# Attention and two MoE layers on one core: a pick made for two tiles at once, a lent token-mix matrix, and a conversion that runs one frame earlier

## The chip, the cores and the metric

The kernel runs on one core of one Trainium2 chip. The metric is device time in microseconds (us). The kernel before took 875.06 us (median of three runs, 874.54 to 876.78).

## What is computed

Sparse attention over 4 batches and 8 heads (576 tokens, 64 wide) keeps the 32 largest scores of a row; a soft mixture of 8 experts and a two-layer MLP follow. Cut to what matters:

```python
scores = q @ k.T / 8                       # per batch and head, 576 x 576
kth    = np.partition(scores, -32)[..., -32]
attn   = softmax(where(scores >= kth, scores, -1e9)) @ v
x      = attn laid out as (2304, 512)
logits = x @ phi                           # 32 slots: 8 experts of 4
slots  = softmax(logits, over tokens).T @ x
out_e  = relu(slots_e @ w1[e]) @ w2[e]     # 8 experts, 512 -> 1024 -> 512
y      = softmax(logits, over slots) @ out_e
h      = y @ w_in                          # 512 -> 2048
g      = h if h >= 1, 0 if h <= -1, else (h + 1)**2 / 4
result = g @ w_out                         # 2048 -> 512
```

## The kernel before

**Stages.** Attention runs over 16 pairs of heads (one pair is two heads of one batch). Then come the experts: `h` (siT times w1, L804), `so` (times w2, L823), the token-mix matrix (`mix`, L757 to L793, written to `cT`), and the MLP (`h_ps` L898, `o_ps` L916).

**A pair** has 1,152 score rows, that is nine tiles of 128 rows: row groups 0 to 3 have two tiles each (j = 0 and 1), row group 4 has one. A tile goes through these steps; a word such as `K31` is step K of row group 3, tile 1.

- S: scores on TensorE (L311) into `s_ps`, of which there are two buffers. C: copy to `ssb` in SBUF on ScalarE (L329).
- G: the eight largest of each of seven segments, on VectorE (L338). L: three rounds on these 56 candidates give the 24 largest in order (L343, L345).
- M: the mask of scores not below the 24th, with a count of them in `cnt_all`. It runs on VectorE (L398), and for the tiles in `MASK_POOL` on GpSimd (L396), whose count ScalarE makes (O, L406).
- X: the scores once more into an `s_ps` buffer (L311), from which a matmul of the mask (L413) takes a huge number wherever the mask is set. Y: the eight largest of what is left (L422, `l`).
- K: the 32nd largest is picked from these eight, by the count. `rank8` holds 31, 30, ..., 24; where it equals the count, the value is kept and summed into `kb`. This is one instruction for a tile, L431, that compares, multiplies and adds up; the sum is fetched by a second one, an accumulator read.
- B (GpSimd, L438), P (ScalarE, L442), U (GpSimd, L445), E (ScalarE, L448) turn the tile into exponentials; T, Q, R, A, H (L457 to L507) transpose it and multiply it by v.

**Order.** The list `ORDER` (L58 to L68) is written by hand and sets the order on TensorE, ScalarE, VectorE and GpSimd through attention. The loop over frames (L710 to L713) emits, for each word, the step of pair frame - k, where the word's last letter gives k (a is 0, b is 1, c is 2). So a frame does the first steps of one pair, the middle steps of the pair before and the last ones of the pair before that. Each pair's step K has nine words; K00 to K11 stand in the pair's own frame, K20 to K40 in the next one. The words `z0` to `z4` prepare the next pair's q and k (copies on ScalarE, differences on GpSimd at L284 and L286, and DMAs). Words `md` and `mc` run pieces of the experts' logits in some frames.

**Conversion.** 16 blocks of w_in are made from 64-bit to 32-bit numbers, one a pair, by the words `c0` to `c6` (ScalarE L213 to L217, GpSimd L219, L223, L225, VectorE L221, load L192, store L205). Their letters are b and c: a pair's block is converted one and two frames after its first steps.

**Weight loads.** 88 loads of 512 KB stand in one list: 64 for w1 and w2, then the converted w_in and w_out. A load needs a free slot in SBUF. At first 13 slots `wA` are free, and each frame may issue two loads (`wload(2)`, at S00). When the last pair begins, six slots of the q and k buffers come free, later others; after the frames the conversion's two (`cv_slots`) and four halves (`half_slots`). What is left waits until `h` and `so` have read a slot: load i takes the slot of an earlier one, in the order of the list `ring`. SP issues all loads, in order.

After the frames, a scheduler orders each engine's work.

Of the kernel before, what the change touches and what calls it, by code (L numbers as in the profile page):

```python
# [8 lines left out]
F32 = mybir.dt.float32  # L9
F32R = mybir.dt.float32r  # L10
# [4 lines left out]
ALU = mybir.AluOpType  # L15
# [4 lines left out]
P = 128  # L20
# [38 lines left out]
Y30b z4b E00b Q30c A11c X21b P11b T40c S00a md M31b H1c A20c Y21b Q31c K20b c4c U01b E01b C00a  # L59
G00a K21b K30b c2c L4b S01a Q40c U11b N3b C01a R4c X31b Y31b A21c E10b S10a T00b T01b G01a B2b  # L60
c5c P21b M40b H2c P20b E11b C10a K31b L0a O40b U21b S11a C11a Q00b A30c N0a B3b M00a X40b G10a
Q01b U20b R0b P30b G11a Y40b L1a M10a A31c T10b S20a H3c T11b c6c E20b E21b R1b N4b S21a M01a
# [3 lines left out]
z3a H0b G31a S40a c0b T30b M21a c1b K11a L3a E40b T31b mc B0a P00a O21a mc c3b R3b C40a  # L66
# [7 lines left out]
def kernel_body(tc, qT, kT, vP, phi, w1, w2, w_in, w_out, out, fast, flag):  # L74
# [8 lines left out]
    cT = cpool.tile([P, NT], F32R, name="cT")  # L83
# [37 lines left out]
    def whole(pool, tag, bufs):  # L121
        return ((pool, tag, bufs),)
# [8 lines left out]
    wfree = list(slots_a)  # L131
# [9 lines left out]
    def wload(n):  # L141
        while n > 0 and wfree and wnext[0] < len(worder):
# [5 lines left out]
            ring.append(slot)  # L148
# [275 lines left out]
    def op_k(u, j):  # L424
        t = st[u]["t0"] + j
        if j == 0:
            st[u]["kb"] = p_small.tile([P, 2], F32, name="kb", tag="kb")
            st[u]["pick"] = p_small.tile([P, 2, 8], F32, name="pick", tag="pick")
        kth = st[u]["kb"][:, j:j + 1]
        if fast:  # L430
            nc.vector.scalar_tensor_tensor(st[u]["pick"][:, j], rank8, cnt_all[:, t:t + 1], st[u]["l8"][:, j],  # L431
                                           op0=ALU.is_equal, op1=ALU.mult, accum_out=kth)
        else:
            nc.vector.tensor_copy(kth, st[u]["top"][:, j, TOPK - 1:])
# [213 lines left out]
    def emit(name, pi):  # L648
        k = name[0]
        if k == "l":  # L650
            op_late(pi, name[1])
        elif k == "z":
            op_split(pi + 1, int(name[1]))
        elif k == "m":
            if pi % NHP == NHP - 1:
                op_moe(pi, k)
        elif k in "cd":
            if k == "c" or pi < NWE:
                i = pi + min(pi, NWE) + (k == "d")
                if i < NCV:  # L660
                    conv_op(i, int(name[1]))
        else:
            if name == "G00" and pi > 0:
                return
            if name == "S00":
                wload(2)
            if pi == NPAIR - 1 and last_pair(name, pi):
                return
            calls[k]((pi, int(name[1])), *([int(name[2])] if len(name) > 2 else []))
            if pi == NPAIR - 1:  # L670
                last_op(name)
# [42 lines left out]
    wfree.extend(cv_slots + half_slots)  # L714
# [41 lines left out]

    def mix():  # L757
        wide = [P, NR + 1, B, NSLOT]
# [20 lines left out]
        for b in range(B):  # L779
# [6 lines left out]
            for rows in (range(NR), (NR,)):  # L786
                ps = ps_m.tile([P, NR, P], F32, name="c_ps", tag="m_ps")
                for r in rows:
                    n = P if r < NR else REM
                    nc.tensor.transpose(ps[:, r % NR, :n], c4[:n, r].rearrange("p a b s -> p (a b s)"), ident[:n, :n])  # L790
                w = len(rows) * n
                nc.scalar.copy(cT[:, b * S + rows[0] * P:b * S + rows[0] * P + w],
                               ps.rearrange("p a b -> p (a b)")[:, :w])  # L793
# [101 lines left out]
    def emit_g(s_):  # L895
        t, f = s_
        ph = ps_m.tile([P, 512], F32, name="h_ps", tag="m_ps")[:, :BLK]
        nc.tensor.matmul(ph, m4[f // 4][:, f % 4 * P:(f % 4 + 1) * P], cT[:, t * BLK:(t + 1) * BLK], start=True, stop=True)  # L898
# [110 lines left out]
```

## Time and profile before

| what | us |
|---|---|
| median of three runs | 875.06 |
| the three runs | 874.54, 876.78, 875.06 |
| span of the profiled execution | 872.0 |
| two startup frames | 0 to 68 |
| frames of the other pairs | 68 to about 527 |
| end of attention, logits of the last batch | 527 to 568.8 |
| experts, mixing, first part of w_out's conversion | 568.8 to 640 |
| rest of the conversion of w_out, first MLP steps | 640 to 710 |
| rest of the MLP | 710 to 872 |

Of the profiled execution only its span is known; the median of the runs is 3.1 us above it (launch and end of the program lie outside the span). Frames are of three kinds: eight plain ones of 31.5 us (from 68.0, 99.6, 131.1, 231.5, 263.0, 363.4, 394.9 and 495.3), three with the words `md` of 35.3 us (from 162.6, 294.5 and 426.4), and three with the words `mc` of 33.6 us (from 197.9, 329.8 and 461.7). The starts named here lie one repeat of TensorE's pattern apart.

### The profile page before, as it was taken

The numbers are of one execution on the slowest core, as the hardware profiler recorded it, in microseconds if no ns is written. First come the engines' busy times: TensorE is split into PE (matmuls) and PEld (weight loads), VectorE is DVE, ScalarE is ACT, GpSimd is POOL, SyncE is SP. The second block draws the span as 40 slices with busy tenths as digits, with TensorE's granted clock in tenths as the row PEclk, the third lists the DMA queues.
The fourth block names the chain that finished last, engine by engine and source line by source line (L and its number), as shares of the span: only waits on it lengthen the run. The fifth ranks groups of instructions, "written<-read, shape, count | busy, mean of one in ns | idle before, by whom it ended". The sixth has DMA issues, their size and how long they took to land.

```text
span 872.0 us, 17711 instructions
## 1 busy us (share of the span) xinstructions
PE 821.5 (94%) x5695; PEld 674.7 (77%) x5695; DVE 685.8 (79%) x3084; ACT 644.8 (74%) x1292; POOL 485.4 (56%) x494
## 2 busy tenths in 40 slices
PE   4889999999999999999999999799698899999996
PEld 3678989988989988988988988632266678888885
DVE  6999999988999989999989994103389995666663
ACT  5688999988998988998988987412578766545453
POOL 2577888877888877888877774100467740000000
PEclk9799999999999999999999999899799999999999
DMA  8453563553353353353452536699940001001001
GB/s 240 124 152 96 165 176 98 156 157 89 103 142 92 112 133 89 102 142 87 117 134 78 157 101 205 206 343 386 399 175 1 0 2 73 37 0 38 1 37 40
DMA packets 49461, 108.59 MB, mean 125 GB/s; under 512 B 8304, under 2 KB 8304, under 8 KB 49360
## 3 DMA queue, kind: packets, MB, share of 16 engines
q1 hardware_dynamic: 49040, 106.73, 40.2%
q8 instruction: 47, 0.77, 0.4%
q10 hardware_dynamic: 320, 0.66, 0.3%
q14 instruction: 54, 0.44, 0.2%
HBM read 70.70 MB, written 8.91 MB: 91 GB/s over the span
## 4 chain that ended last, share of the span: by engine, by line
PE 78%; DVE 10%; DMA 6%; ACT 3%; POOL 1%; issue 1%; ACTq 0%; POOLq 0%; SPq 0%; DVEq 0%
PE s_ps L311 20%; PE o_ps L916 17%; PE av_ps L485 14%; PE pt_ps L457 7%; PE s_ps L413 4%; PE av_ps L486 3%; PE rem_ps L230 3%; DMA w<-in_moe_w_dram 2%; DMA w<-in_moe_w_out_dram 2%; PE h L804 2%; DVE cand L338 2%; PE moe_ps L569 2%; DMA w<-cv_d 1%; PE h_ps L898 1%; PE xT_ps L534 1%
## 5 line engine op out<-in xcount | busy, mean ns | idle before, releaser
L311 PE MATMUL s_ps<-kh,q 128*128 128x288 f32 x640 | 208.1, 342 | 16.4 <-DVE q L266 9.0
L916 PE MATMUL o_ps<-whl,ghl 128*128 128x512 f32 x864 | 216.9, 395 | 5.0 <-DVE ghl L904 4.0
L916 PEld LDWEIGHTS o_ps<-whl,ghl 128*128 128x128 f32 x864 | 159.1, 188 | 44.7 <-DVE ghl L904 7.1
L445 POOL TENSOR_TENSOR ssb<-ssb,pen 128x576 f32<-128x576 f32 x141 | 180.4, 1284 | 18.3 <-ACT pen L442 15.8
L311 PE MATMUL s_ps<-kl,q 128*128 128x288 f32 x640 | 181.2, 299 | 0.0
L338 DVE MAX8 cand<-ssb 128x8 f32<-128x82 f32 (+1 forms) x1008 | 164.2, 228 | 5.0 <-ACT ssb L329 4.0
L311 PEld LDWEIGHTS s_ps<-kh,q 128*128 128x128 f32 x640 | 123.6, 193 | 34.7 <-DVE q L266 9.4
L485 PE MATMUL av_ps<-v_sb,ptb 128*128 128x65 f32 (+1 forms) x1280 | 147.1, 261 | 0.4 <-ACT xT L547 0.4
L485 PEld LDWEIGHTS av_ps<-v_sb,ptb 128*128 128x128 f32 (+1 forms) x1280 | 141.1, 181 | 5.2 <-issue 2.6
L311 PEld LDWEIGHTS s_ps<-kl,q 128*128 128x128 f32 x640 | 124.4, 194 | 0.3
L422 DVE MAX8 l<-s_ps 128x8 f32<-128x576 f32 x144 | 109.2, 758 | 18.3 <-PE s_ps L413 17.9
L442 ACT ACTIVATE pen<-ssb,kb 128x576 bf16<-128x576 f32 x141 | 110.3, 792 | 4.5 <-POOL kb L438 3.3
L329 ACT COPY ssb<-s_ps 128x576 f32<-128x576 f32 x144 | 91.1, 641 | 25.3 <-PE s_ps L311 21.8
L448 ACT ACTIVATE ssb<-ssb,nm 128x576 f32<-128x576 f32 x141 | 109.0, 785 | 0.6 <-POOL ssb L445 0.6
L900 ACT ACTIVATE rg<-h_ps,half 128x384 f32<-128x384 f32 x96 | 55.2, 579 | 71.0 <-PE h_ps L898 70.8
L396 POOL TENSOR_SCALAR mb<-ssb,top 128x576 bf16<-128x576 f32 x48 | 83.3, 1736 | 19.2 <-DVE top L345 9.2
L902 DVE SCALAR_TENSOR_TENSOR rg<-h_ps,rg 128x384 f32<-128x384 f32 x96 | 52.9, 554 | 47.4 <-ACT rg L901 47.1
L467 ACT COPY ptb<-pt_ps 128x512 f32<-128x512 f32 x144 | 82.4, 598 | 3.3 <-PE av_ps L485 3.3
L457 PE MATMUL pt_ps<-ident,ssb 128*128 128x128 f32 x576 | 84.3, 273 | 0.2
L398 DVE TENSOR_SCALAR_CACHE_REDUCE mb<-ssb,top 128x576 bf16<-128x576 f32 x96 | 75.8, 802 | 0.0
L345 DVE MAX8 top<-cand 128x8 f32<-128x56 f32 x432 | 73.5, 207 | 0.1
L457 PEld LDWEIGHTS pt_ps<-ident,ssb 128*128 128x128 f32 x576 | 68.7, 142 | 1.3 <-ACT ptb L467 0.8
(160 smaller groups left out, 1311.7 us busy)
## 6 DMA issues: line engine op xcount, KB each, us to landing
w<-in_moe_w_dram SPq DMA_DIRECT2D x60, 512.0 KB, 6.7
q<-qst SPq DMA_DIRECT2D x60, 160.0 KB, 3.1
kh<-kst SPq DMA_DIRECT2D x60, 144.0 KB, 2.5
kl<-kst SPq DMA_DIRECT2D x60, 144.0 KB, 2.9
x<-in_moe_w_in_dram SPq DMA_DIRECT2D x16, 512.0 KB, 3.9
w<-in_moe_w_out_dram SPq DMA_DIRECT2D x16, 512.0 KB, 9.3
v_sb<-in_v_dram SPq DMA_DIRECT2D x16, 325.0 KB, 2.9
raw_t<-in_q_dram SPq DMA_DIRECT2D x15, 320.0 KB, 3.7
```

The source lines that it names most:

```text
L311: nc.tensor.matmul(s[:, hf, :HS], a, w, start=(n == 0), stop=(n == len(terms) - 1), skip_group_check=True)
L329: nc.scalar.copy(st[u]["ssb"][:, j], st.pop((u, j))[:, :, :HS])
L338: nc.vector.max(st[u]["cand"][:, j, 8 * g:8 * g + 8], row(u, j)[:, S * g // NSEG:S * (g + 1) // NSEG])
L396: nc.gpsimd.tensor_scalar(st[u]["mb"][:, j], row(u, j), t_u, None, op0=ALU.is_ge)
L422: nc.vector.max(st[u]["l8"][:, j], st.pop((u, j))[:, :, :HS])
L442: nc.scalar.activation(pen, row(u, j), AF.Relu, bias=st[u]["kb"][:, j:j + 1], scale=-BIG)
L445: nc.gpsimd.tensor_tensor(row(u, j), row(u, j), st.pop((u, "pen", j)), op=ALU.subtract)
L448: nc.scalar.activation(row(u, j), row(u, j), AF.Exp, bias=st[u]["nm"][:, j:j + 1], scale=0.125)
L457: nc.tensor.transpose(pt[:, c, :], pr[:, c * P:(c + 1) * P], ident)
L467: nc.scalar.copy(ptb, st.pop((u, "pt", j)))
L485: nc.tensor.matmul(o, pj[:, c, sl], v_sb[:, 4 * jj + c, :], start=(c == 0), stop=False)
L916: nc.tensor.matmul(pos[t][n], a[:, sl], w, start=(f == 0 and k == 0), stop=(f == NF - 1 and k == 2))
```

## The change

Four edits.

- **Pick.** `op_k` does nothing for the first tile of a row group. At the group's last tile it picks for both: a compare of `rank8` with the counts (128x16), a multiply by `l8` (128x16), and a sum over each tile's eight (128x2). Three instructions, the second and third of which use what the one before wrote. Row group 4 has one tile and takes three instructions too (128x8). Per pair, nine picks of two instructions each (18) become five of three (15).
- **Lent matrix.** `cT`, 9 KB a partition, was allocated for the whole kernel and is written by `mix` only. It becomes two tiles in a pool of its own, which are two more slots for the first two weight loads. They are not put in `ring`.
- **Conversion one frame earlier.** The letters of c0, c1 and c3 change from b to a, those of c2, c4, c5 and c6 from c to b.
- **Slots of the conversion.** `cv_slots` are given to weight loads after the last block's c6, which now stands in the last pair's next frame, instead of after all frames.

```diff
-G00a K21b K30b c2c L4b S01a Q40c ...     (c4c c5c c6c c2c -> b; c0b c1b c3b -> a)
+G00a K21b K30b c2b L4b S01a Q40c ...
...
-    cT = cpool.tile([P, NT], F32R, name="cT")
+    p_ct = ctx.enter_context(tc.tile_pool(name="p_ct", bufs=1))
...
-    wfree = list(slots_a)
+    loan = [whole(p_ct, f"cT{n}", 1) for n in range(2)]
+    wfree = loan + slots_a
...
-            ring.append(slot)
+            if slot not in loan:
+                ring.append(slot)
...
     def op_k(u, j):
-        t = st[u]["t0"] + j
-        if j == 0:
-            st[u]["kb"] = p_small.tile([P, 2], F32, name="kb", tag="kb")
-            st[u]["pick"] = p_small.tile([P, 2, 8], F32, name="pick", tag="pick")
-        kth = st[u]["kb"][:, j:j + 1]
+        n, t = width[u[1]], st[u]["t0"]
+        if j < n - 1:
+            return
+        kb = st[u]["kb"] = p_small.tile([P, 2], F32, name="kb", tag="kb")
         if fast:
-            nc.vector.scalar_tensor_tensor(st[u]["pick"][:, j], rank8, cnt_all[:, t:t + 1], st[u]["l8"][:, j],
-                                           op0=ALU.is_equal, op1=ALU.mult, accum_out=kth)
+            pick = p_small.tile([P, 2, 8], F32, name="pick", tag="pick")[:, :n]
+            wide = [P, n, 8]
+            nc.vector.tensor_tensor(pick, rank8.unsqueeze(1).to_broadcast(wide),
+                                    cnt_all[:, t:t + n].unsqueeze(2).to_broadcast(wide), op=ALU.is_equal)
+            nc.vector.tensor_tensor(pick, pick, st[u]["l8"][:, :n], op=ALU.mult)
+            nc.vector.reduce_sum(kb[:, :n], pick, axis=AX.X)
...
                     conv_op(i, int(name[1]))
+                    if (i, name[1]) == (NCV - 1, "6"):
+                        wfree.extend(cv_slots)
+                        wload(99)
...
-    wfree.extend(cv_slots + half_slots)
+    wfree.extend(half_slots)
...
+        cT.extend(p_ct.tile([P, NT // 2], F32R, name=f"cT{n}", tag=f"cT{n}", bufs=1) for n in range(2))
...
-        ph = ...; nc.tensor.matmul(ph, m4[...], cT[:, t * BLK:(t + 1) * BLK], ...)
+        ph = ...; nc.tensor.matmul(ph, m4[...], cT[t // 3][:, t % 3 * BLK:(t % 3 + 1) * BLK], ...)
```

The line numbers of the changed kernel are two higher from L141 on (L338 is L340, L398 is L400, L422 is L424), and the pick's three instructions are L434, L436 and L437.

**Where instructions move, on VectorE.** The place is the second half of a frame, from the L2 selection (three `MAX top` and two pairs of `MATCH_REPLACE`) to the mask M30 (L398, the second one below). Before:

```order
L345 MAX top<-cand 128x8 x2
L431 SCALAR_TENSOR_TENSOR pick,kb<-rank_77,cnt_all,l_1262 128x8
L338 MAX cand<-ssb 128x8 x7
L398 TENSOR_SCALAR mb,cnt_all<-ssb,top 128x576
L431 SCALAR_TENSOR_TENSOR pick,kb<-rank_77,cnt_all,l_1317 128x8
L422 MAX l_1317<-s_ps 128x8
L338 MAX cand<-ssb 128x8 x7
L431 SCALAR_TENSOR_TENSOR pick,kb<-rank_77,cnt_all,l_1317 128x8
L345 MAX top<-cand 128x8 x2
```

And now:

```order
L347 MAX top<-cand 128x8 x2
L434 TENSOR_TENSOR pick<-rank_79,cnt_all 128x16
L436 TENSOR_TENSOR pick<-pick,l_1288 128x16
L437 TENSOR_REDUCE kb<-pick 128x2
L340 MAX cand<-ssb 128x8 x7
L400 TENSOR_SCALAR mb,cnt_all<-ssb,top 128x576
L424 MAX l_1340<-s_ps 128x8
L340 MAX cand<-ssb 128x8 x7
L434 TENSOR_TENSOR pick<-rank_79,cnt_all 128x16
L436 TENSOR_TENSOR pick<-pick,l_1340 128x16
L437 TENSOR_REDUCE kb<-pick 128x2
L347 MAX top<-cand 128x8 x2
```

K01 and K11 are three instructions each where there was one with its accumulator read, and K10, ahead of the MAX of Y11 (`l_1317`), is gone.

**On SP's queue of DMAs**, around the start of a pair in the middle of attention, where the first 13 slots run out. `raw_t` is the next pair's k and q, `lall` the logits, `x` the next block to convert, `cv_d` a converted block, `w` a weight load. Before:

```order
L250 DMA raw_t<-in_k_dram 128x576
L251 DMA raw_t<-in_q_dram 128x640
L167 DMA w_3238<-in_moe_w_dram 128x1024
L574 DMA lall<-lT 32x576
L192 DMA x_3272<-in_moe_w_in_dram 128x1024
L205 DMA cv_d_101<-tr 128x512
```

And now:

```order
L252 DMA raw_t<-in_k_dram 128x576
L253 DMA raw_t<-in_q_dram 128x640
L169 DMA w_3284<-in_moe_w_dram 128x1024
L169 DMA w_3286<-in_moe_w_dram 128x1024
L581 DMA lall<-lT 32x576
L194 DMA x_3318<-in_moe_w_in_dram 128x1024
L207 DMA cv_d_104<-tr 128x512
```

The thirteenth load before stood alone in its frame; now it has a fourteenth beside it, and a fifteenth follows in the next frame.

## Rows read from the trace of the kernel before

**Rows 1.** The page: busy time of two engines, and the chain that ended last, by engine.

```profile
PE 821.5 (94%) x5695; PEld 674.7 (77%) x5695; DVE 685.8 (79%) x3084; ACT 644.8 (74%) x1292; POOL 485.4 (56%) x494
...
PE 78%; DVE 10%; DMA 6%; ACT 3%; POOL 1%; issue 1%; ACTq 0%; POOLq 0%; SPq 0%; DVEq 0%
```

**Rows 2.** Busy time of each engine in a stretch: the stretch, its length, busy us (instructions) of each engine, then TensorE's granted clock, the share of the DMA engines and GB/s. Two startup frames, a plain frame, the last plain frame, one frame with `md` and one with `mc`.

```profile
0.00:36.50 36.50, 21.11 (x87) 16.34 (x87) 29.07 (x165) 17.71 (x32) 13.29 (x20) 0.86 0.78 216
36.50:68.00 31.50, 27.35 (x200) 23.40 (x201) 31.19 (x175) 27.69 (x53) 23.49 (x27) 1.00 0.43 113
...
99.55:131.07 31.52, 31.52 (x257) 28.36 (x257) 30.31 (x170) 29.06 (x60) 26.55 (x29) 1.00 0.53 148
...
495.31:526.83 31.52, 31.52 (x258) 28.29 (x258) 29.27 (x171) 28.35 (x60) 23.12 (x27) 1.00 0.28 88
162.59:197.90 35.31, 35.31 (x274) 31.34 (x273) 31.20 (x172) 30.87 (x64) 27.23 (x29) 1.00 0.43 120
197.90:231.48 33.58, 33.58 (x313) 29.91 (x312) 30.62 (x172) 29.96 (x63) 26.61 (x29) 1.00 0.40 109
```

**Rows 3.** The timeline of VectorE in the plain frame from 99.55, from the pick K01 to the accumulator read of M30: start, us, engine, line, what, count (some rows hold several instructions).

```profile
119.75 0.24 DVE L431 SCALAR_TENSOR_TENSOR pick<-rank,cnt_all,l 128x8 f32<-128x8 f32 x1
...
119.92 1.11 DVE L338 MAX8 cand<-ssb 128x8 f32<-128x82 f32 x7
...
121.67 0.22 DVE L431 SCALAR_TENSOR_TENSOR pick<-rank,cnt_all,l 128x8 f32<-128x8 f32 x1
...
121.82 0.76 DVE L422 MAX8 l<-s_ps 128x8 f32<-128x576 f32 x1
122.50 1.10 DVE L338 MAX8 cand<-ssb 128x8 f32<-128x82 f32 x7
123.52 0.20 DVE L431 SCALAR_TENSOR_TENSOR pick<-rank,cnt_all,l 128x8 f32<-128x8 f32 x1
...
123.65 0.33 DVE L345 MAX8 top<-cand 128x8 f32<-128x56 f32 x2
...
125.23 0.81 DVE L398 TENSOR_SCALAR_CACHE_REDUCE mb<-ssb,top 128x576 bf16<-128x576 f32 x1
125.97 0.08 DVE L398 DVE_READ_ACCUMULATOR mb<-ssb,top 128x1 f32 x1
```

**Rows 4.** TensorE and then its weight loads at the end of that stretch: the last score matmul of X30 and the mask matmul behind it.

```profile
125.83 0.29 PE L311 MATMUL s_ps<-kl,q 128*128 128x288 f32 x1
126.10 0.41 PE L413 MATMUL s_ps<-mb,nbig 128*128 128x288 bf16 x2
...
125.96 0.24 PEld L413 LDWEIGHTS <-nbig 128*128 128x128 bf16 x2
```

**Rows 5.** GpSimd at the same place: the difference for q, then the mask M21.

```profile
118.42 1.54 POOL L286 TENSOR_TENSOR qst<-raw_t,qst 128x640 fp32r<-128x640 f32 x1 [0.67 <-ACT qst L282]
120.00 1.74 POOL L396 TENSOR_SCALAR mb<-ssb,top 128x576 bf16<-128x576 f32 x1
```

**Rows 6.** Small VectorE instructions behind one another: two picks in a row in the first frame, two pairs in which the second uses the first's result, and the TENSOR_TENSOR of L784 (its line: duration ns min/median/max).

```profile
36.29 0.21 DVE L431 SCALAR_TENSOR_TENSOR pick<-rank,cnt_all,l 128x8 f32<-128x8 f32 x1
...
36.43 0.22 DVE L431 SCALAR_TENSOR_TENSOR pick<-rank,cnt_all,l 128x8 f32<-128x8 f32 x1
...
537.90 0.17 DVE L517 TENSOR_SCALAR den<-xu 128x9 f32<-128x9 f32 x1 [3.22 <-ACT xu L498]
538.11 0.21 DVE L518 RECIPROCAL den<-den 128x9 f32<-128x9 f32 x1
...
L784 DVE TENSOR_TENSOR c<-lt,ch x4: 484/492/493, 605.2 to 608.5; 128x320 f32<-128x320 f32 x4
```

**Rows 7.** Picks and other VectorE instructions with two inputs in SBUF, beside GpSimd: the picks of the whole run (duration ns min/median/max), a pick and the GpSimd instruction at its side, and the same for one of the MLP's.

```profile
L431 DVE SCALAR_TENSOR_TENSOR pick<-rank,cnt_all,l x144: 198/220/1457, 22.4 to 534.4; 128x8 f32<-128x8 f32 x144
...
51.47 1.46 DVE L431 SCALAR_TENSOR_TENSOR pick<-rank,cnt_all,l 128x8 f32<-128x8 f32 x1
...
51.49 1.42 POOL L284 TENSOR_TENSOR kst<-raw_t,kst 128x576 fp32r<-128x576 f32 x1
...
656.56 0.56 DVE L905 TENSOR_TENSOR ghl<-rg,ghl 128x384 fp32r<-128x384 f32 x1
...
655.53 1.49 POOL L219 TENSOR_SCALAR tr_l<-tr_l 128x512 f32<-128x512 f32 x1 [1.35 <-ACT tr_l L213]
```

**Rows 8.** The same place as in rows 3 and 4 in a frame with `mc` (from 197.90) and one with `md` (from 162.59): the accumulator read of M30, and TensorE's mask matmul.

```profile
225.35 0.08 DVE L398 DVE_READ_ACCUMULATOR mb<-ssb,top 128x1 f32 x1
...
189.05 0.08 DVE L398 DVE_READ_ACCUMULATOR mb<-ssb,top 128x1 f32 x1
...
226.49 0.30 PE L413 MATMUL s_ps<-mb,nbig 128*128 128x288 bf16 x1
...
192.92 0.30 PE L413 MATMUL s_ps<-mb,nbig 128*128 128x288 bf16 x1
```

**Rows 9.** Stretches behind the frames, columns as in rows 2: the end of the last block's conversion, and the experts with the mixing. Then, of the chain of waits, its two longest pieces in that last stretch (start, us, what).

```profile
546.00:550.00 4.00, 3.45 (x29) 2.89 (x28) 0.67 (x3) 1.66 (x6) 1.92 (x2) 1.00 0.40 131
...
568.77:640.40 71.63, 61.40 (x362) 21.50 (x362) 21.20 (x42) 25.88 (x50) 14.26 (x11) 0.93 1.04 390
...
588.92 10.78 DMA w<-in_moe_w_dram
599.77 10.87 DMA w<-in_moe_w_dram
```

More of the change, by code (lines that the diff above doesn't have):

```diff
@@ L58 @@
 ORDER = '''
[L59 to L62, printed above, removed]
+Y30b z4b E00b Q30c A11c X21b P11b T40c S00a md M31b H1c A20c Y21b Q31c K20b c4b U01b E01b C00a
+G00a K21b K30b c2b L4b S01a Q40c U11b N3b C01a R4c X31b Y31b A21c E10b S10a T00b T01b G01a B2b
+c5b P21b M40b H2c P20b E11b C10a K31b L0a O40b U21b S11a C11a Q00b A30c N0a B3b M00a X40b G10a
+Q01b U20b R0b P30b G11a Y40b L1a M10a A31c T10b S20a H3c T11b c6b E20b E21b R1b N4b S21a M01a
 C20a M11a A40c C21a Q10b A41c U30b N1a K40b H4c B4b X00a S30a Q11b P31b lDc Y00a T20b md G20a
@@ L65 @@
 U31b z1a lCc Y01a X11a E31b mc C31a Q20b L2a K01a Q21b G30a M20a z2a K10a md U40b Y11a md
-z3a H0b G31a S40a c0b T30b M21a c1b K11a L3a E40b T31b mc B0a P00a O21a mc c3b R3b C40a
+z3a H0b G31a S40a c0a T30b M21a c1a K11a L3a E40b T31b mc B0a P00a O21a mc c3a R3b C40a
 B1a X20a M30a P10a mc U00a U10a mc P01a N2a Y20a G40a A10b X30a
@@ L424, in op_k @@
     def op_k(u, j):
-        t = st[u]["t0"] + j
-        if j == 0:
-            st[u]["kb"] = p_small.tile([P, 2], F32, name="kb", tag="kb")
-            st[u]["pick"] = p_small.tile([P, 2, 8], F32, name="pick", tag="pick")
-        kth = st[u]["kb"][:, j:j + 1]
-        if fast:
-            nc.vector.scalar_tensor_tensor(st[u]["pick"][:, j], rank8, cnt_all[:, t:t + 1], st[u]["l8"][:, j],
-                                           op0=ALU.is_equal, op1=ALU.mult, accum_out=kth)
+        n, t = width[u[1]], st[u]["t0"]
+        if j < n - 1:
+            return
+        kb = st[u]["kb"] = p_small.tile([P, 2], F32, name="kb", tag="kb")
+        if fast:
+            pick = p_small.tile([P, 2, 8], F32, name="pick", tag="pick")[:, :n]
[4 more added lines that the diff above has]
+            nc.vector.reduce_sum(kb[:, :n], pick, axis=AX.X)
         else:
-            nc.vector.tensor_copy(kth, st[u]["top"][:, j, TOPK - 1:])
+            nc.vector.tensor_copy(kb[:, :n], st[u]["top"][:, :n, TOPK - 1])
     def op_b(u):
@@ L755, in mix_tile @@
         return t.rearrange(f"p ({' '.join(axes)}) -> p {' '.join(axes)}", **dict(zip(axes, shape[1:])))
+    cT = []
     def mix():
+        cT.extend(p_ct.tile([P, NT // 2], F32R, name=f"cT{n}", tag=f"cT{n}", bufs=1) for n in range(2))
         wide = [P, NR + 1, B, NSLOT]
@@ L791, in mix @@
                 w = len(rows) * n
-                nc.scalar.copy(cT[:, b * S + rows[0] * P:b * S + rows[0] * P + w],
+                nc.scalar.copy(cT[b // 2][:, b % 2 * S + rows[0] * P:b % 2 * S + rows[0] * P + w],
                                ps.rearrange("p a b -> p (a b)")[:, :w])
@@ L897, in emit_g @@
         ph = ps_m.tile([P, 512], F32, name="h_ps", tag="m_ps")[:, :BLK]
-        nc.tensor.matmul(ph, m4[f // 4][:, f % 4 * P:(f % 4 + 1) * P], cT[:, t * BLK:(t + 1) * BLK], start=True, stop=True)
+        nc.tensor.matmul(ph, m4[f // 4][:, f % 4 * P:(f % 4 + 1) * P], cT[t // 3][:, t % 3 * BLK:(t % 3 + 1) * BLK], start=True, stop=True)
         r, g = (x[:, :BLK] for x in ring_tile("g", g_slots, "rg", F32))
```

## The prediction

> **What bounds the kernel now.** The page comes first: TensorE is busy 94% of the span and makes up 78% of the chain that ended last, VectorE 10%, DMA 6% [rows 1]. Those are averages, so the stretches come next. A plain frame of 31.52 us has TensorE busy all of its 31.52 us, and VectorE 30.3 [rows 2]. By this view TensorE bounds the frame, and 1.2 us more on VectorE would be free. The timeline says otherwise at one place. From K01 at 119.75 VectorE runs without a gap through G30, M20, K10, Y11, G31, K11 and the L3 selection to the mask M30, whose accumulator read starts at 125.97 [rows 3]. TensorE starts the last score matmul of X30 at 125.83, 0.13 after the one before as usual, but the mask matmul that needs M30 only at 126.10 and not at about 125.96 [rows 4]. So TensorE already waits for this chain, by some 0.14, and the chain has **no slack**: what is added between 119.75 and 125.23 lengthens the frame. The 1.2 us that VectorE idles lie ahead of this chain (it waits for the X01 scores), so they can't pay for it. The same wait stands in all eight plain frames. In a frame with `mc` M30 is there at 225.43 and TensorE comes at 226.49, a slack of 1.06; in one with `md` it is 192.92 - 189.13 = 3.8 [rows 8]. In the first two frames VectorE itself is the bound (29.07 of 36.5, 31.19 of 31.5 [rows 2]). Behind attention, from 568.77 to 640.40, the DMA engines are full (share 1.04, 390 GB/s), and the chain runs over weight loads [rows 9].
>
> **The pick: what one costs.** Three picks in a row in front of nothing else would start 36.43 - 36.29 = 0.14 to 0.15 apart, accumulator read included: they don't use each other's results [rows 6]. In the chain, K01 takes 0.17, K10 0.15 and K11 0.13 [rows 3]; I take 0.147 for each, 0.29 for two. The three new instructions do depend on each other. Rows with such a dependence: 537.90 to 538.11, 0.21 for 128x9 [rows 6]. A 128x16 TENSOR_TENSOR isn't in the trace. Below it, as an own bound, is the pick's own 0.198 at the least; above it L784 (128x320) with 0.484 to 0.493 [rows 6, 7], and 16 elements lie near the lower end. So a start-to-start of 0.2 for the compare, 0.2 for the multiply, and 0.08 to 0.11 until an independent instruction can follow the sum (picks overlap their followers by 0.05 to 0.07): **0.50 for a group**, bounds 0.42 (all three at a pick's spacing) and 0.63 (three times 0.21). Against two picks that is +0.21; for row group 4, with one tile, +0.35.
>
> **What lies on the path in a plain frame.** K01 becomes a group: +0.36. K10 goes: -0.15. K11 becomes a group: +0.36. Sum **+0.57**. The rest has cover: K21, K31 and K40 and the empty K00, K20, K30 lie between 126 and the X01 scores of the next frame, where VectorE's 1.2 idle us absorb their +0.21, +0.21 + 0.35 less the two waits below. B of a group starts no earlier than before, since kb for both tiles was complete at the second pick anyway.
>
> **A lock on top.** Picks wait for GpSimd: the shortest takes 0.198 us, the longest 1.457 [rows 7]. The pick at 51.47 lasts exactly as long as L284 on GpSimd, which began at about the same time. A TENSOR_TENSOR of GpSimd thus keeps a VectorE instruction with two SBUF inputs out for its whole length. Its TENSOR_SCALAR does not: L219 runs from 655.53 to 657.02, and the L905 that starts at 656.56 has its normal 0.56. (Behind the start of an L219 others are late by 0.3 to 0.5.) I estimate from these that it blocks its first 0.57 us for 512 elements, 0.64 for 576. In a plain frame GpSimd ends L286 at 119.96 and starts M21's L396 (576 elements) at 120.00 [rows 5]. K01 now slips in at 119.75. After the change the compare takes that place, and the multiply, also with two SBUF inputs, wants to start at 119.95 to 120.03, just when L396 does. If it loses, the chain pays up to another **0.64**. Bounds: 0 and, if the whole L396 counts, 1.74. I take 0.64, because the multiply depends on the compare, which can't end before 119.95, and L286's end and the start of L396 leave a gap of 0.04 only. The removed K00 gives back such a wait too (51.47: 1.46 instead of 0.2), but outside the chain in plain frames.
>
> [...]
>
> **Sum over attention.** Seven plain frames at +0.57 + 0.64 = +1.21: 8.5. The last plain frame (from 495.31) has two GpSimd instructions fewer (27 for 29 [rows 2]), M21 begins earlier there and the lock doesn't strike: +0.56. Frames with `mc`: 1.21 less the slack 1.06, about +0.2 with spread, three times: +0.6. Frames with `md`: slack 3.8, 0. Startup frame 0 (picks K00 to K11): -0.15 + 0.36 + 0.64 - 0.15 + 0.36 = +1.05. Startup frame 1 (five groups): four times +0.21, +0.35 for K40, +0.64, less the wait of 1.26 that goes with K00 [rows 7]: +0.57. Together **+11.3**.
>
> **The lent matrix.** From 568.77 to 640.40 the DMA engines carry 390 GB/s [rows 9], 27.9 MB or 53 loads, 1.34 us each. Two loads more are issued in attention, in frames where the DMA share is 0.40 to 0.53 [rows 2], behind the next pair's q and k on SP's queue, so nothing waits for them. So two fewer stand in the saturated stretch: **-2.7**. The bounds are 0 (if the chain there, in which the loads of 588.92 and 599.77 wait for slots [rows 9], is set by slots alone) and -2.7. cT is written by `mix` long after loads 0 and 1 have been read.
>
> **Conversion and its slots.** The same seven instructions of a block move past S00 to S11 of a frame, and load and store move with them. In plain frames each word stays at its place in the list, so the count per frame is the same: 0. Startup frames get one block's instructions on GpSimd and ScalarE (13.3 and 17.7 of 36.5 busy [rows 2]) and one VectorE shift: under 0.2. The last block's vanish from 544 to 552, where TensorE is at 3.45 of 4 [rows 9]: at most -0.5, in a stretch that its own chain of pen, subtract and exp sets; I take 0. The two slots given back earlier start two loads earlier in a stretch with a DMA share of 0.40 [rows 9]; the full stretch starts when `h` reads slots, and I take 0 (bound -2.7, as above).
>
> **Tail order.** The scheduler orders the MLP anew; the work is the same. Bound: 2 to 5 us either way, I take 0.
>
> **How the numbers follow.** Against the profiled execution the sum is 872.0 + 11.3 - 2.7 = 880.6; the median of the runs lies 3.1 above its span, so **883.7** (+1.0%). What a measurement of this kernel can tell from no change is about 0.3%, 2.6 us.
>
> - **Forecast** (0.50): the group costs 0.50 and the multiply is caught by L396: 883.7, by the size of the group's bounds 880.5 to 887.
> - **Rival 1, no lock** (0.25): the multiply gets in ahead of L396, or that starts later. 8 frames at 0.57, startup +0.4, `mc` 0: +5.0 - 2.7 = +2.3, 877.4. For it: GpSimd may move with the longer frame. Against: the gap of 0.04.
> - **Rival 2, faster** (0.10): the price of a pick goes by the number of instructions, 15 for 18, and dependence costs nothing, so K01 + K10 + K11 cost no more than now and only the two loads remain: 872.4. It decides at a group of 0.29 or less. Against it: 0.147 between independent picks and 0.21 between dependent ones [rows 6]. [...]
> - **Rival 3, whole lock** (0.05): L396 keeps the multiply out for all its 1.74: 1.1 more in seven plain and 1.1 in three `mc` frames and at startup, about +12: 896.
> - **Rival 4, tail** (0.10): the new order of the MLP moves the end by 2 to 5 us, either way; around no lock and lock half each, 875 to 889.
>
> The range is 875.5 to 888.5: it holds the forecast, rival 1 and most of rival 4, and leaves out rivals 2 and 3. Faster by over 0.3%: 0.06 of rival 2 and 0.04 of rival 4, 0.10. Within 0.3%: the smaller half of rival 2, 0.15 of rival 1, a little of rival 4, 0.20. Slower: 0.70.
>
> **What would show it.** Right, if plain frames last 32.1 to 32.9 us, K01's multiply lasts 0.7 to 0.9 instead of 0.2 beside an L396, and the mask matmul of X30 waits for M30 by over a microsecond; and if the stretch behind the last frame is 2 to 3 us shorter with the DMA engines as full. Wrong, if plain frames stay at 31.5 (then a dependent trio is as cheap as two picks, or M30 got in front some other way), if the wait shows at another place, for instance X01 or X21, or if the tail moves by more than 4 us.

## The result, and the profile after

The changed kernel takes **887.62 us** (median of four runs, 886.89 to 891.17) against 875.92 for the kernel before on the same chip: a ratio of 1.0131, 95% interval 1.0102 to 1.016. The forecast was 883.7, with a range of 875.5 to 888.5: it has the direction, the time lies in its range, and the loss is 11.7 us where 8.6 were forecast. The profiled execution's span is 885.0 us against 872.0. As the sections below show, the sum came near because two of its terms were wrong in opposite directions: attention lost less than forecast, and what stands behind it lost much where a gain was forecast.

The page of the changed kernel, busy time and chain by engine, which answer to [rows 1]:

```profile
PE 827.3 (93%) x5695; PEld 679.9 (77%) x5695; DVE 695.6 (79%) x3036; ACT 647.0 (73%) x1292; POOL 484.3 (55%) x494
...
PE 69%; DVE 20%; ACT 3%; issue 3%; POOL 2%; DMA 1%; ACTq 0%; SPq 0%; POOLq 0%; DVEq 0%
```

VectorE's share of the chain has doubled to 20%: in the plain frames it now ends the waits. DMA's share is down from 6% to 1%: between 568 and 640 the chain before ran over weight loads for 51 us, and the one of the changed kernel runs over none there.

Its stretches, columns as in [rows 2]: the two startup frames, a plain frame, the experts to the last weight load, the stretch from the first part of w_out that is ready to the last (`whl`, L903), and the rest:

```profile
0.00:37.70 37.70, 20.95 (x88) 16.45 (x89) 29.80 (x163) 19.21 (x35) 14.79 (x21) 0.88 0.77 209
37.70:70.50 32.80, 30.29 (x199) 25.99 (x198) 30.10 (x166) 27.81 (x54) 26.92 (x29) 0.88 0.47 133
102.71:134.88 32.17, 31.58 (x259) 28.39 (x258) 30.63 (x167) 29.22 (x60) 26.60 (x29) 1.00 0.52 146
576.12:647.70 71.58, 62.09 (x363) 21.75 (x364) 21.31 (x43) 25.00 (x48) 14.63 (x11) 0.94 1.02 380
633.60:720.11 86.51, 73.27 (x287) 50.25 (x287) 74.13 (x110) 62.89 (x116) 58.74 (x43) 0.95 0.17 68
720.11:885.01 164.90, 158.07 (x703) 130.64 (x701) 102.37 (x210) 84.25 (x155) 0.00 (x0) 0.99 0.08 30
```

The last two stretches in the kernel before:

```profile
624.84:713.96 89.12, 78.57 (x316) 53.90 (x317) 76.65 (x122) 68.04 (x126) 60.91 (x43) 0.95 0.20 77
713.96:872.01 158.05, 151.22 (x674) 125.19 (x672) 96.78 (x200) 80.10 (x148) 0.00 (x0) 0.99 0.08 31
```

Where the 13.0 us of the two spans are: the experts start at 576.12 instead of 568.77, +7.35. Of that, pair 2's first mask matmul comes 2.7 later (16.37 + 33.05 + 34.19 = 83.61 against 80.91; these are the first one of pair 0 and the steps from pair to pair), and the eight plain frames are 0.61 longer each, 4.9; the frames with `md` and `mc` have kept their 35.28 and 33.57; the end of attention is 0.2 shorter. From the start of the experts to the first `whl` it is 57.48 against 56.07, +1.4 (its first step alone is 2.7 longer, at a granted clock of 0.86 instead of 1.00: last section); from there to the last `whl` 86.51 against 89.12, -2.6; and from there to the end 164.90 against 158.05, **+6.9**. The last number is explained by the column of TensorE's instructions: 287 instead of 316 were done while w_out was prepared, so 703 instead of 674 are left. These 29 are 26 `o_ps` matmuls and 3 `h_ps` (counted in the trace: 231 of 864 `o_ps` done at the last `whl`, against 257).

### The profile page after: what moved, and what is told of

The parts are those of the page before. It is cut to its first block, busy times and chain, and to the rows that moved or that the text cites. A ratio compares the mean times of both kernels' runs of the same rounds, so it can differ in the third digit from the quotient of the medians.

```text
span 885.0 us, 17694 instructions
## 1 busy us (share of the span) xinstructions
PE 827.3 (93%) x5695; PEld 679.9 (77%) x5695; DVE 695.6 (79%) x3036; ACT 647.0 (73%) x1292; POOL 484.3 (55%) x494
## 4 chain that ended last, share of the span: by engine, by line
PE 69%; DVE 20%; ACT 3%; issue 3%; POOL 2%; DMA 1%; ACTq 0%; SPq 0%; POOLq 0%; DVEq 0%
PE o_ps L927 18%; PE s_ps L313 15%; PE av_ps L490 11%; PE pt_ps L462 5%; DVE cand L340 4%; PE s_ps L415 3%; PE av_ps L491 3%; DVE mb L400 3%; PE rem_ps L232 2%; DVE top L347 2%; DVE cand L345 2%; PE h L815 2%; DVE l L424 2%; PE moe_ps L574 2%; PE so L834 2%
## 5 line engine op out<-in xcount | busy, mean ns | idle before, releaser
L927 PEld LDWEIGHTS o_ps<-whl,ghl 128*128 128x128 f32 x864 | 161.5, 189 | 42.9 <-DVE ghl L915 6.3
L450 POOL TENSOR_TENSOR ssb<-ssb,pen 128x576 f32<-128x576 f32 x141 | 181.1, 1289 | 9.6 <-ACT pen L447 6.7
L340 DVE MAX8 cand<-ssb 128x8 f32<-128x82 f32 (+1 forms) x1008 | 164.5, 230 | 5.0 <-ACT ssb L331 4.3
L424 DVE MAX8 l<-s_ps 128x8 f32<-128x576 f32 x144 | 109.0, 757 | 19.8 <-PE s_ps L415 19.3
L398 POOL TENSOR_SCALAR mb<-ssb,top 128x576 bf16<-128x576 f32 x48 | 83.4, 1738 | 13.9 <-DVE pick L434 5.2
L400 DVE TENSOR_SCALAR_CACHE_REDUCE mb<-ssb,top 128x576 bf16<-128x576 f32 x96 | 75.9, 804 | 0.3 <-POOL ssb L450 0.3
L221 POOL TENSOR_SCALAR tr_l<-tr_l 128x512 f32<-128x512 f32 x16 | 25.2, 1575 | 85.0 <-PE soT_ps L842 77.5
```

What stands on the lines that cost most here:

```text
L340: nc.vector.max(st[u]["cand"][:, j, 8 * g:8 * g + 8], row(u, j)[:, S * g // NSEG:S * (g + 1) // NSEG])
L400: nc.vector.tensor_scalar(st[u]["mb"][:, j], row(u, j), t_u, 0.0, op0=ALU.is_ge, op1=ALU.add, accum_out=cnt_all[:, t:t + 1])
L424: nc.vector.max(st[u]["l8"][:, j], st.pop((u, j))[:, :, :HS])
L450: nc.gpsimd.tensor_tensor(row(u, j), row(u, j), st.pop((u, "pen", j)), op=ALU.subtract)
L927: nc.tensor.matmul(pos[t][n], a[:, sl], w, start=(f == 0 and k == 0), stop=(f == NF - 1 and k == 2))
```

## The chain in a plain frame

The cause in attention can be read in a plain frame. VectorE in the one from 102.71, the place of [rows 3]:

```profile
123.06 0.26 DVE L434 TENSOR_TENSOR pick<-rank,cnt_all 128x16 f32<-128x16 f32 x1
123.34 0.17 DVE L436 TENSOR_TENSOR pick<-pick,l 128x16 f32<-128x16 f32 x1
123.56 0.17 DVE L437 TENSOR_REDUCE kb<-pick 128x2 f32<-128x16 f32 x1
123.64 1.11 DVE L340 MAX8 cand<-ssb 128x8 f32<-128x82 f32 x7
...
127.08 0.16 DVE L434 TENSOR_TENSOR pick<-rank,cnt_all 128x16 f32<-128x16 f32 x1
127.28 0.17 DVE L436 TENSOR_TENSOR pick<-pick,l 128x16 f32<-128x16 f32 x1
127.49 0.17 DVE L437 TENSOR_REDUCE kb<-pick 128x2 f32<-128x16 f32 x1
127.58 0.33 DVE L347 MAX8 top<-cand 128x8 f32<-128x56 f32 x2
...
129.89 0.08 DVE L400 DVE_READ_ACCUMULATOR mb<-ssb,top 128x1 f32 x1
```

TensorE at the end of that chain, the place of [rows 4]:

```profile
129.14 0.29 PE L313 MATMUL s_ps<-kl,q 128*128 128x288 f32 x1
130.03 0.41 PE L415 MATMUL s_ps<-mb,nbig 128*128 128x288 bf16 x2 [0.59 <-DVE mb L400]
```

GpSimd beside it, the place of [rows 5]:

```profile
121.73 1.55 POOL L288 TENSOR_TENSOR qst<-raw_t,qst 128x640 fp32r<-128x640 f32 x1 [0.20 <-ACT qst L284]
123.31 1.73 POOL L398 TENSOR_SCALAR mb<-ssb,top 128x576 bf16<-128x576 f32 x1
```

What to see: the group K11 takes 127.58 - 127.08 = 0.50, its three starts 0.20 and 0.21 apart. K01 takes 0.58, since its compare waits for the end of L288 (123.28) and lasts 0.26 instead of 0.16. Its multiply starts at 123.34, 0.03 after L398 began, and lasts 0.17: L398 doesn't hold it. TensorE's wait for M30 is 0.59. The sum of K01 (+0.41), the missing K10 (-0.15) and K11 (+0.37) is +0.63, against 0.61 measured. The followers of the sum speak for the dependence as the price: the MAX behind it, which doesn't use it, starts 0.08 to 0.09 after it, while in K11 the multiply and the sum, each of which uses the result before it, start 0.20 and 0.21 behind that. No run has the same three without the dependence.

## Experiments

Each is timed in five rounds beside the kernel before on the same chip, and the ratio is to that. "Tail" means the stretch from the start of the experts to the end.

**One edit at a time.** The kernel before with the new `op_k` alone (`e1_pick`); with `cT` lent alone (`e2_loan`); with the conversion's seven letters and its slots given after the last c6 (`e3_conv`); and the changed kernel with the old `op_k` (`e4_loan_conv`).

```diff
 e1_pick       op_k as changed; nothing else
 e2_loan       +    loan = [whole(p_ct, f"cT{n}", 1) for n in range(2)]
               +    wfree = loan + slots_a          (and cT in two tiles)
 e3_conv       c4c c2c c5c c6c c0b c1b c3b -> c4b c2b c5b c6b c0a c1a c3a
               +                        wfree.extend(cv_slots); wload(99)
 e4_loan_conv  e2_loan and e3_conv together
```

> The kernel before with the pick for two tiles alone. Theory P (the dependent trio costs 0.50 us against 0.147 for a pick and lengthens the chain to M30 in the eight plain frames, the lock of L396 does not strike): plain frames 32.1 instead of 31.5, frames with md and mc as before, so +4.9 at the start of the experts, and up to +1.5 more in the two startup frames. Rival S (the lengthening of the frames comes from the conversion's GpSimd work, one frame earlier): plain frames 31.5. The tail is planned anew here too; theory T (the tail's order after 640 us is worth some 5 us either way, whichever edit changes it) lets the time differ from +5 to +6 by up to 6 us, the rival (the order costs nothing, what was lost behind attention came from the loan or the conversion) gives 880 to 882.

> The kernel before with the lent token-mix matrix alone. Attention as before (plain frames 31.5, experts start at 568.8). Theory L (two loads fewer in the saturated stretch): the last weight load lands 2.7 us earlier than before's 640.4; then -2.7 or, if the new order of the tail costs what it cost in the changed kernel, +2 to +3. [...]

> The kernel before with the conversion one frame earlier and its slots given back in the last frame. Theory S1 (the conversion's GpSimd instructions of the first block now stand among the first pair's steps, 1.5 us at 28.8 and 1.3 us at 38.3 in the changed kernel): the first two frames longer by about 1.2 us, plain frames 31.5, so +1.2 at the experts, less at most 0.5 at the end of attention. Rival (startup is lost to the pick): no change up to the experts. The tail is planned anew: plus or minus 5.

> The changed kernel with the picks of before: loan and conversion alone. If attention is as the sum of the two (startup +1.2, frames as before) and the two loads bring 2.7, it is 873 to 874 with a tail order as good as before's, and 878 to 880 with one as poor as the changed kernel's. If it beats the kernel before, the pick alone is what costs.

| run | us (median) | ratio, 95% interval | pair 2's first mask matmul | experts start | from there to the end | `o_ps` done at the last `whl` |
|---|---|---|---|---|---|---|
| before (profile, span 872.0) | | | 80.9 | 568.8 | 303.2 | 257 |
| e1_pick | 892.74 | 1.0172 (1.0148 to 1.0196) | 81.7 | 574.4 | 312.9 | 231 |
| e2_loan | 886.89 | 1.0101 (1.0079 to 1.0123) | 81.1 | 569.0 | 316.3 | 210 |
| e3_conv | 883.65 | 1.0061 (1.0037 to 1.0085) | 81.0 | 572.2 | 311.1 | 240 |
| e4_loan_conv | 886.78 | 1.0100 (1.0075 to 1.0125) | 81.5 | 569.3 | 315.6 | 213 |
| changed kernel | 887.62 | 1.0131 (1.0102 to 1.016) | 83.6 | 576.1 | 308.9 | 231 |

Theory P holds: plain frames last 32.1 with the pick and 31.5 without it, in every run. S1 falls: the conversion alone doesn't lengthen the first two frames. Every edit alone, the loan included, gives a tail that is 8 to 13 us longer, and the three losses don't add up: 1.7%, 1.0% and 0.6% alone, 1.3% together. That fits theory T, a new order, but the order had not been touched by itself yet. Of the longer tails, 1.9 to 2.3 us in e1, e3 and e4 are a first step of the experts at a lower clock (0.64 in e1 from 575 to 580; last section); e2, at 1.00 there, has no such part. That the experts start 3.4 us later in e3, although its frames are those of before, goes with the clock too: from 552.3 to 562.3, at the end of attention, the granted clock is 0.50 there, and 0.97 before. The loan alone, its stretches from the first to the last `whl` and to the end:

```profile
626.61:715.19 88.58, 73.73 (x263) 47.93 (x261) 67.85 (x104) 61.08 (x111) 58.58 (x43) 0.88 0.15 60
715.19:885.30 170.11, 163.19 (x725) 134.86 (x723) 105.71 (x217) 86.92 (x160) 0.00 (x0) 0.99 0.08 29
```

TensorE has 263 instructions done at the last `whl`, 53 fewer than before, and the rest takes 170.1 us instead of 158.05, 12 more.

**The order by itself.** The scheduler's order of an engine can be held by edges that only say "issue behind" between the instructions behind the frames. `f1_pick_tail_of_before` is the pick alone with the order of the kernel before on TensorE, VectorE, ScalarE and GpSimd; `f2_before_tail_of_pick` is the kernel before with the order that the scheduler made for the pick alone.

```diff
+TAIL = {'PE': '-116 0:1 -115:-99 ...', 'DVE': ..., 'Activation': ..., 'Pool': ...}   # places in the order as written
...
+    for eng, text in TAIL.items():
+        ...
+        for a, z in zip(order, order[1:]):
+            tc.add_manual_dep(mine[k0 + z][1], mine[k0 + a][1].name, NoSync, reason="pinned")
```

> The pick alone, with the four compute engines behind attention held to the order of the kernel before. Theory O (the loss behind attention is the order that the scheduler chose anew): from the start of the experts to the end it takes what the kernel before takes, 303 us in the profile and not 313 as in the pick alone, so the whole is the attention's +5.6 to +6.5 and 881 to 884 against 877. Rival (the pick's changed attention itself costs later, by the clock or by where the loads stand): still 890 or more.

> The kernel before, with the four compute engines behind attention held to the order that the scheduler chose for the pick alone. Theory O: attention as before and the tail of the pick alone (313 us instead of 303), 885 to 888. Rival: as before, 875 to 878.

Measured: f1 882.98 us, ratio **1.0051** (1.0031 to 1.007); f2 887.09 us, ratio **1.0113** (1.0087 to 1.0139). So the pick alone costs 0.5% with the order of before and 1.7% with its own, and the order alone costs the kernel before 1.1%. Theory O is shown for this pair of orders, from both sides. One number of the expectation for f1 missed: its tail is 307.0 us and not 303. The 4 us lie ahead of the first `whl` (60.6 for 56.1), where the first step takes 2.5 longer and, from 615.4 to 622.2, the granted clock is 0.50. From the first to the last `whl`, and from there to the end, first f1:

```profile
636.83:725.12 88.29, 78.95 (x316) 56.59 (x317) 76.12 (x122) 68.14 (x126) 60.10 (x43) 0.93 0.15 61
725.12:883.23 158.11, 151.28 (x674) 125.24 (x672) 96.84 (x200) 80.12 (x148) 0.00 (x0) 0.99 0.08 31
```

And f2:

```profile
628.10:719.62 91.52, 78.03 (x284) 54.36 (x280) 70.14 (x109) 61.33 (x115) 59.06 (x43) 0.88 0.16 65
719.62:884.01 164.39, 157.55 (x701) 130.35 (x700) 101.86 (x209) 84.47 (x155) 0.00 (x0) 0.99 0.08 30
```

The order decides how much of the MLP's activation gets done beside the preparation of w_out (122 instructions of VectorE against 109) and so how many matmuls TensorE gets done in that time (316 against 284). The preparation takes 88 us in f1 and 92 in f2, 3.2 longer; and what TensorE didn't do then it does afterwards, when it is the bound, busy for 151.28 of the 158.11 us in f1: 316 - 284 = 32 instructions fewer, 6.3 us more.

**Part of the order.** `f3_lc_tail_of_before` (loan and conversion) and `f4_after_tail_of_before` (the changed kernel) hold TensorE and GpSimd to the order of before, VectorE only from its 39th instruction of the MLP and ScalarE only in the conversion of w_out.

```diff
+TAIL = {'PE': <all from m_first on>, 'Pool': <all>, 'DVE': <from the 39th of the MLP>, 'Activation': <L213, L215, L217, L891>}
```

> Loan and conversion, without the pick, TensorE and GpSimd behind the experts held to the order of the kernel before, VectorE from its 39th instruction on, ScalarE in the conversion of w_out. Theory O with theory L (two loads fewer are worth up to 2.7 us): 874 to 877, equal to the kernel before or up to 0.3% faster. Rival (loan and conversion cost by themselves): 885 or more, as loan and conversion with their own order.

> The changed kernel, held to the same orders as the run before. Theory O: attention +7.3 as in the changed kernel, the tail about 296 to 300 from the start of the experts to the last matmul instead of 302: 880 to 885. Rival: 887 to 889 as the changed kernel.

Measured: f3 889.76 us, 1.0142 (1.0116 to 1.0167); f4 895.55 us, 1.02 (1.0178 to 1.0222). Both expectations missed. From the first to the last `whl` f3 needs 101 us instead of 89, with as many TensorE instructions done:

```profile
626.58:727.74 101.16, 77.63 (x315) 54.92 (x315) 71.70 (x120) 67.37 (x122) 59.52 (x43) 0.90 0.15 61
```

In f4 it is 102 us. A likely reason is that parts of one plan's order, mixed with parts of another's, make engines wait for each other; this wasn't shown. So these two runs say nothing about the loan.

**Ring and order held.** The loan also turns the ring: since two loads no longer take a slot of it, each later load, and each buffer of the MLP behind it, stands two slots further on. `g1_loan_aligned` turns it back by these two, gives the loan alone and holds all four engines to the order of before. `g2_lc_aligned` adds the conversion one frame earlier, with its slots given back after the frames as before; `g3_after_aligned` adds the new pick to that.

```diff
+    ring = ring[2:] + ring[:2]
     while wnext[0] < len(worder):
         wfree.append(ring.pop(0))
...
-    wfree.extend(half_slots)              (g2, g3: as before)
+    wfree.extend(cv_slots + half_slots)
```

> The loan alone, with two things held as in the kernel before: the ring of slots is turned by the two loads that the loan takes, so that each later load stands in the slot of before, and the four compute engines behind attention keep the order of before. Theory O + L (loan saves two loads in the full stretch, the rest was the order): the last weight load starts 2.0 us sooner after the start of the experts than before's 64.4, and the kernel is 0 to 2.5 us faster than the kernel before. Rival (the loan costs by itself, for instance by slots that come free later): as slow as the loan alone with its own order, 8 to 10 us slower.

> Loan and conversion one frame earlier, the conversion's two slots given back after the frames as before, ring and order held as in the run before. Theory: as that run, within 1 us (the conversion costs and brings nothing); 0 to 2.5 us faster than the kernel before. Rival (the conversion lengthens the first two frames by 1.2 us): 1 us slower than that run.

> The same with the pick of the change: the changed kernel but for when the conversion's slots are given back, ring and order behind attention held as before. Theory: the pick's frames alone remain, +4.9 in the plain frames and +1 to +2.7 in the first two, less the loan's 0 to 2.5: 880 to 884 where the kernel before has 877. Rival (the tail of the changed kernel is slow for another reason than ring and order): 887 or more.

Measured: g1 877.96 us, 1.0009 (0.9987 to 1.0031); g2 877.69 us, 1.001 (0.999 to 1.003); g3 885.65 us, 1.012 (1.0081 to 1.016). The loan that cost 1.0% with its own order and ring costs nothing measurable with those of before, and brings nothing measurable either. Which of the two, ring or order, cost it wasn't separated. The conversion neither costs nor brings. g3's median lies above what was expected; its runs are spread widely, from 882.8 to 894.1, and the spread goes with the granted clock: 0.959 and 0.966 in the two longest, with spans of 892.2 and 888.2, and 0.971 to 0.979 in the other four, with 880.7 to 884.0. In its profile (span 880.7, +8.7) attention has lost 7.3 us and the tail, 304.6 us against 303.2, another 1.4. So in the profile the tail is no longer the changed kernel's 308.9, as the theory has it; what lowered the clock in the two long runs, and with them the ratio, isn't known. By the median alone g3 can't be told from the changed kernel. Its last two stretches are those of the kernel before:

```profile
633.54:722.54 89.00, 78.47 (x316) 53.89 (x317) 76.60 (x123) 68.04 (x126) 60.89 (x43) 0.96 0.18 72
722.54:880.71 158.17, 151.25 (x674) 125.16 (x672) 96.78 (x200) 80.10 (x148) 0.00 (x0) 0.99 0.08 31
```

**The conversion with late slots.** `h1_conv_slots_late` moves the seven words only and holds nothing.

```diff
 c4c c2c c5c c6c c0b c1b c3b -> c4b c2b c5b c6b c0a c1a c3a    (cv_slots after the frames, as before)
```

> The conversion one frame earlier and nothing else: its two slots are given back after the frames, as before, and nothing is pinned. Built so, the scheduler gives the four compute engines behind attention the very order of the kernel before. Theory O: as the kernel before, within 0.3%, with 31 activation steps and 257 o_ps matmuls done when the last part of w_out is prepared. Rival (the conversion alone, with its slots given early, was 0.6% slower because its instructions are in the way earlier): 0.6% slower again.

Measured: 878.83 us, ratio 1.0004 (0.9983 to 1.0024); span 872.1, 257 `o_ps` done at the last `whl`, tail 303.2. With the slots given back earlier (e3) the same edit was 0.6% slower. It is the moment at which two slots come free, and the order that followed, that cost there.

**All traces together.** In the eight traces in which TensorE has the order of before through the MLP (before, f1, f3, f4, g1, g2, g3, h1), with and without the pick, the loan and the earlier conversion, 257 `o_ps` are done at the last `whl` and the rest takes 158.0 to 158.4 us. In the six with another order (the changed kernel, e1 to e4, f2) 210 to 240 are done, and the rest takes 162.2 to 170.1: about 0.25 us more for each one that is left. The granted clock doesn't decide it: between the first and the last `whl` it is 0.93 in f1, with 257 done, and 0.95 in the changed kernel, with 231.

## Why the forecast came out as it did

**The chain without slack: right.** Adding to VectorE between K01 and M30 lengthened all eight plain frames and no other: 0.61 each, against the forecast's own +0.57 for the picks (rival 1's figure). The frames with `mc` and their slack of 1.06 took it without a loss. The rest had its cover too, as forecast: at the start of a frame an instruction of a group still takes 0.89 to 1.30 instead of 0.16 or 0.17 and ends 0.02 to 0.04 after GpSimd's L450, which has two inputs (15 groups), and this doesn't lengthen the frames.

**The price of the trio: right.** 0.50 was forecast, 0.50 measured for K11. Three that depend on each other start 0.20 to 0.21 apart here, where independent picks start 0.14 to 0.15 apart with the accumulator read [rows 6]. Rival 2 is out: 15 instructions cost more than 18.

**The lock of L396: the step that failed in attention.** The forecast said that "the multiply ... wants to start at 119.95 to 120.03, just when L396 does. If it loses, the chain pays up to another 0.64". It did come to stand there, 0.03 to 0.05 us behind the start of the mask in seven plain frames, and was not held by it in any (0.17 or 0.18 us). That takes 0.64 from seven frames, 4.5 us, from the forecast, and the 0.2 for each `mc` frame. The mask does hold such an instruction when it comes 0.2 later (0.56 us instead of 0.16: last section), so it was the moment that the forecast had wrong: the multiply still gets in. Rival 3, the whole lock, is out with it, and attention came out nearest to rival 1, no lock: the multiply takes its usual 0.17 inside the mask's 1.73. Beside a GpSimd instruction with two inputs the compare does wait: the one at 123.06 takes 0.26 instead of 0.16 and ends at 123.32, 0.04 after L288. But the forecast's "for its whole length" isn't what every such row shows. Of 14 compares that start 0.00 to 0.04 behind an L450 in the changed kernel, seven last 1.28 to 1.30, and seven 0.16; behind these seven it is the multiply that lasts 1.14 or 1.15.

**Startup: too small.** +1.62 was forecast, 1.28 of it from the lock, which didn't strike; the changed kernel has +2.7. Pair 2's first mask matmul came at 80.3 to 81.5 in nine profiles without the pick, at 81.7 in e1, and at 83.5 to 83.7 in the other four with it (the changed kernel, f1, f4, g3). So the loss isn't the conversion's. But e1 and f1 have the same frames and lie 2.0 apart. Here is TensorE's clock near the end of the second frame, first in e1, then in f1:

```profile
66.00:69.00 3.00, 3.00 (x26) 2.70 (x25) 2.85 (x13) 2.00 (x5) 1.42 (x4) 1.00 0.15 55
66.00:69.00 3.00, 3.00 (x14) 2.19 (x13) 2.81 (x8) 1.27 (x3) 1.49 (x3) 0.50 0.44 176
```

In the same 3 us it is 0.52 in the changed kernel and 1.00 in the kernel before; from 36 to 70 it is 0.86 in f1 and in the changed kernel, 0.95 in e1 and 1.00 in the kernel before. So some 2 us of the 2.7 go with the clock. Whether the pick brings the fall about isn't shown; what is left to it, 0.8 in e1, is hardly more than the profiles without it differ among themselves. In sum attention lost 7.35 where 11.3 were forecast.

**The loan's -2.7: mis-sized, and it doesn't reach the end.** From the start of the experts to the issue of the last weight load it is 64.4 us before and 62.1 with the loan alone, both with a first step of 17.06 us: a gain of 2.2. The changed kernel (63.6) and g1 (64.8) have slower first steps, of 19.7 and 19.6. Four runs without the loan whose first step takes 18.4 to 19.5 (e1, e3, f1, f2) need 65.5 to 65.9. So the loads are about 2 us sooner in the changed kernel too, and with the ring turned back about 1. In the run with the loan alone `so` ends 1.9 us sooner (612.8 for 614.7), but the next step, `m_ps`, starts at 616.77 in both, because in the new order TensorE does the last transposes of the mix (`c_ps`) ahead of those of `so`. So sooner loads didn't make a shorter tail: with ring and order of before g1's is 307.1 us, with a slow first step, and f1's, without the loan and with a first step as slow, is 307.0. The bound of 0 that was kept for this term is what the runs g1 and g2 show.

**Tail order, "the work is the same ... I take 0": the step that failed most.** Its bound was 2 to 5 us either way, with a chance of 0.10 for that rival. Measured: +1.1% for the order alone (f2), 6.9 us between the last `whl` and the end in the changed kernel, and 5.7 over its whole tail (308.9 for 303.2), beyond the 4 us that the prediction had named as a sign of being wrong. The amount of work was the same; when it was done was not. Nor did it go either way: the scheduler made another order for each of the changed kernel, e1, e2, e3 and e4, and each had fewer matmuls done (210 to 240 for 257). Why the order of the kernel before is better than all of these stays open. That the number came near is luck: 4 us too much in attention, 8 us too little behind.

## What to carry to other kernels

Count in dependent steps, not in instructions: merging two picks into three short instructions that wait for each other was slower here, by 0.61 us a plain frame, and it cost time just where the chain had no slack, although the engine had 1.2 us to spare in the frame as a whole. Where a scheduler orders a later stage, compare its order before and after for a number that matters there (here: matmuls done when the last weight is ready), as an edit elsewhere can cost more through it than through itself. Before blaming or praising an edit, hold the order and the buffers behind it: the loan that seemed to cost 1.0% cost 0.1%, within the noise, once order and ring were held. And before a profile is compared with another, compare the granted clock of their stretches.

## What the runs showed of the hardware that was not expected

**When GpSimd's mask holds VectorE.** The multiply that starts 0.03 us behind L398 isn't held (0.17 us), but a compare that starts 0.21 behind one is (0.56 us instead of 0.16). VectorE and then GpSimd at 535:

```profile
535.78 0.56 DVE L434 TENSOR_TENSOR pick<-rank,cnt_all 128x16 f32<-128x16 f32 x1
...
535.57 1.73 POOL L398 TENSOR_SCALAR mb<-ssb,top 128x576 bf16<-128x576 f32 x1
```

It ends at 536.34, 0.77 after the start of L398, and 0.96 before its end. The same compare stands in the other four traces with the pick (e1, f1, f4, g3), 0.20 or 0.21 behind the mask, and again takes 0.56 and ends 0.77 after its start. The kernel before has a pick that starts 0.48 behind a mask; it takes 0.28 instead of 0.20 to 0.22, and ends 0.76 after the mask's start, as in the other eight traces without the new pick:

```profile
528.26 0.28 DVE L431 SCALAR_TENSOR_TENSOR pick<-rank,cnt_all,l 128x8 f32<-128x8 f32 x1
...
527.78 1.73 POOL L396 TENSOR_SCALAR mb<-ssb,top 128x576 bf16<-128x576 f32 x1
```

So in these rows an instruction that starts 0.03 to 0.05 behind the mask isn't held, and one that starts 0.20 to 0.48 behind it is, and ends 0.76 to 0.77 after the mask's start, 0.96 or 0.97 before its end. It is the same place of the program in each of the five traces, and in each of the nine.

**TensorE's clock at the start of the experts.** The 144 matmuls of the first step took 17.06 us before, in e2 and in h1, 19.73 in the changed kernel, 18.47 in f2 and 19.56 in g1; e2, f2, g1 and h1 have plain frames as long as those of the kernel before. First before, then the changed kernel, 4 us each ahead of the start, and the first step:

```profile
560.00:564.00 4.00, 1.10 (x8) 0.90 (x8) 1.80 (x6) 1.40 (x5) 0.00 (x0) 0.71 0.99 343
564.00:568.00 4.00, 2.79 (x52) 2.29 (x52) 0.46 (x2) 0.62 (x3) 0.00 (x0) 0.50 0.40 151
568.77:585.83 17.06, 17.06 (x144) 5.47 (x148) 1.70 (x4) 2.06 (x3) 0.00 (x0) 1.00 1.03 372
```

```profile
567.50:571.50 4.00, 1.02 (x9) 0.85 (x9) 1.74 (x5) 1.48 (x5) 0.00 (x0) 0.97 0.10 37
571.50:575.50 4.00, 2.79 (x51) 2.26 (x51) 0.51 (x2) 0.63 (x3) 0.00 (x0) 0.50 0.01 4
576.12:595.85 19.73, 19.73 (x144) 5.78 (x148) 1.70 (x4) 2.06 (x3) 0.00 (x0) 0.86 0.98 347
```

TensorE is busy for 1.10 and 1.02 us of the first 4 us, and in the next 4 us the granted clock is 0.50 in both. In the kernel before it is 0.71 already in the first 4 us, and 1.00 in the first step; in the changed kernel it is 0.97 in the first 4 us, still 0.50 from 575.5 to 579.5, and 0.86 over the first step. What makes it fall isn't shown. Frames of the same lengths gave both cases, so these 2.7 us shouldn't be credited to an edit. Each kernel has one trace only, so that they move from run to run of one kernel isn't shown directly; but in 23 runs of the kernel before beside g1, g2 and g3 the granted clock over the whole span goes from 0.984 to 0.968, and the span from 871.9 to 879.4 us with it.
